# One core, a long convolution beside a token-mixing MLP: order of the sine table, taps in one evacuation, inverse table after the last gelu, even products in place

## The chip, the cores and the metric

The kernel runs on one core of a Trainium2 chip. The metric is the device time of one execution in microseconds (us), lower is better. Engines are named as in the profile: PE (matrix multiply), PEld (its weight loads), DVE (vector), ACT (activation), POOL (GpSimd), SP (the queue that issues most transfers).

## What is computed

Sequence length S = 2048, width D = 640, F = 1536, bf16 inputs. Path A is an H3-like layer: a short causal convolution of k (4 taps per channel), times v, then a long convolution over the sequence with one filter per channel (written with FFTs), plus a skip term, times q. Path B is a layer norm of x = q over D, a two-layer MLP over the sequence axis with a tanh-gelu, and a transpose back. A gate per token, g = sigmoid(sum(x * gate_w)), blends them.

```python
k_shift = sum over t of k_pad[:, t:t + S, :] * shift_k[:, ks - 1 - t]
kv = k_shift * v
y  = irfft(rfft(kv padded to 2S) * rfft(ssm_k padded to 2S))[:S] + kv * ssm_D
a  = q * y
u  = gelu(einsum("bsd,sf->bdf", layernorm(x), w1) + b1)
b  = (einsum("bdf,fs->bds", u, w2) + b2) transposed
out = g * a + (1 - g) * b
```

## The kernel before

**Long convolution.** It is done with real trigonometric tables and matrix products. The sequence is split in two halves h and, inside each, in four residues p. The table FTB (slices p = 0 to 3, 128x1024 each) holds sines and cosines. The arguments are made by integer arithmetic on DVE into `pint` (L791 to L796: a product, an add of 1024, an AND with 4095, for each p in the order 0, 2, 1, 3) and go through `Sin` on ACT (L797). `pint` lies on the memory of ring[1]; the k tiles `kn` and `kp` use the same bytes later.

**Filter.** `transp(h, db)` (L826) turns the filter block by block on PE against an identity; ACT evacuates each block into `wT` (L837). The skip term ssm_D is folded in by one row product per block (Drow). Then `fwd` (L839) multiplies `wT` by the table for each p, and ACT evacuates into C[0] (h = 0) and C[1] (h = 1). `mixing` (L869) combines the four residues on DVE.

**Short convolution.** The taps are laid out by a DVE copy "taps" (L789) from the small load `rows`, transposed by four tiny PE products (L808 to L810), and copied into `cw` by four ACT instructions, one per group of 32 partitions (L812). POOL multiplies `cw` with a mask `m32` into the shift table KF (L944, four instructions). k is turned by transposing DMAs into KT, and `kv` (L971) multiplies KT by KF on PE; the result times v is the signal.

**Signal.** `fwd_even` (L853) transforms the signal's residues p = 0 and 2: eight PE products, each evacuated by ACT ("Ae", L861) into a temporary buffer Th, from which three DVE instructions (L865 to L867) make all slots of the target for p = 0 and 2. `fwd` does p = 1 and 3. The signal's first half goes to C[2] with C[1] as the temporary (L999), the second to C[3] with C[2] (L1006). C[1] holds the filter's second half until its mixing is done.

**MLP.** Layer-norm statistics on DVE, their power step on POOL (L904 to L908), the normalisation on DVE (L913). m1 products (L1025 on) accumulate over the sequence for 12 column tiles ft; ACT applies the gelu into GT (L1039). m2 products (L1065 on) are evacuated by ACT into O1 (L1084).

**Inverse.** The inverse table is made from FTB: four transposing DMAs into GTB (L1060), then four ACT copies in place over FTB (L1061, "gil"). Spectral products run on DVE (`cross`, `product`), then `invmix`, and `inverse` (L1171) on PE, whose evacuation and the blend with O1 end the kernel.

**What sets the order.** Nothing is ordered by hand. Every instruction is added to `_Sched` (L324) with an engine, an estimated duration and a priority (its index in program order unless `prio` is given; lower goes first). `run` (L384) simulates the engines with these estimates and takes, on each free engine, the ready instruction with the lowest priority number. `emit` then issues in that order, and each engine runs its own list strictly in order. A dependency is found from overlapping memory regions; `after` lets an operation be taken only once another has started in the simulation. An evacuation's dependencies are handed to the first PE product of its group (L370 to L376). PSUM is cut into four slots of two banks; MLP groups may hold two of them, convolution groups three. SP, ACT ("QA") and POOL issue transfers; most on SP are chained in program order.

```python
            if e in ("SP", "QA") or op.lat < 0:
                issue = 1.2 if e == "POOL" else 0.1
                s = max(t + issue, dma_free)
                dma_free = s + op.dur
                op.end = dma_free + 2.0 + (6.0 if e == "POOL" else 0.0)
```

Of the kernel before, what the change touches and what calls it, by code (L numbers as in the profile page):

```python
# [323 lines left out]
class _Sched:  # L324
# [59 lines left out]
    def run(self):  # L384
# [12 lines left out]
        pend = {e: [] for e in engs}  # L397
        free = {e: 0.0 for e in engs}
        port = {"DVE": 0.0, "POOL": 0.0}
# [111 lines left out]
def _build(nc, A_q, A_k, A_v, A_shift_k, A_ssm_k, A_ssm_D, B_x, B_w1, B_b1, B_w2, B_b2, gate_w, out):  # L511
# [10 lines left out]
    with ExitStack() as es:  # L522
# [13 lines left out]
        def alloc(name, shape, dtype, at=None):  # L536
            size = mybir.dt.size(dtype)
            for s_ in shape[1:]:
                size *= s_
            if at is None:  # L540
                off = cur[0]
                cur[0] = (off + size + 63) // 64 * 64
            else:
                off = at
            assert off % 4 == 0 and off + size <= top, f"SBUF overflow {name}: {off}+{size} > {top}"
            h = nc.alloc_sbuf_tensor_at(name, list(shape), dtype, offset=off)
            T.reg_sbuf(h, off)
            return h
# [46 lines left out]
        ksh = [alloc(f"ksh{i}", [128, 4, D], BF16, at=base_of(GT) + 5120 * (1 + i)) for i in range(2)]  # L595
        rows = alloc("rows", [20, 4, 512], BF16, at=base_of(GT))
        kn = [alloc(f"kn{i}", [128, 4, D], BF16, at=base_of(ring[1]) + 5120 * i) for i in range(2)]
# [21 lines left out]

        def tt(eng, o, a, b, op, mode=2, prio=None):  # L620
            n = n_of(o)
            d = dve_dur(n, mode) if eng == "DVE" else n / 600.0 + 0.17
            o_ = SC.add(eng, d, lambda s: T.op(eng, lambda e: e.tensor_tensor(o, a, b, op), [a, b], [o]),  # L623
                        [a, b], [o], prio=prio, name="tt")
            o_.lock = True
            return o_
# [138 lines left out]
        small(Drow[:, :], dr(A_ssm_D, 0, [[0, 1], [1, D]]), 1280, "QA")  # L765
        small(rows[0:20, 0, 0:128], dr(A_shift_k, 0, [[128, 20], [1, 128]]), 5120, "QA")
        small(rows[0:4, 1, :], dr(B_b2, 0, [[512, 4], [1, 512]]), 4096, "QA")
        small(rows[0:12, 2, 0:128], dr(B_b1, 0, [[128, 12], [1, 128]]), 3072, "QA")
        for a, b in SSM0:
            ssm_load(0, a, b)  # L770
        for hk in range(4):
            x_load(hk)
        for a, b in SSM1:
            ssm_load(1, a, b)
# [11 lines left out]
        ts("DVE", ident[:, :], dif[:, :], 0.0, None, ALU.is_equal)  # L786
        memset("POOL", cw[:, :, :], 0.0)
        ro, ri = rows[0:20, 3, :].rearrange("g (j q c) -> g j q c", j=4, q=4), V(rows, 0, [[1, 4], [0, 4], [4, 32]], pn=20)
        SC.add("DVE", 0.6, lambda s: T.op("DVE", lambda e: e.tensor_copy(ro, ri), [ri], [ro]), [ri], [ro], prio=0, name="taps")  # L789
        PORD = (0, 2, 1, 3)  # L790
        for p in PORD:  # L791
            pv = pint[:, p, :, 1, :]
            tt("DVE", pv, V(acol, p, [[4, 2], [0, 256]]), V(brow, 0, [[0, 2], [1, 256]]), ALU.mult, mode=1)
            ts("DVE", pint[:, p, :, 0, :], pv, 1024.0, None, ALU.add, mode=2)
            pa = pint[:, p, :, :, :].rearrange("q a b c -> q (a b c)")
            ts("DVE", pa, pa, 4095, None, ALU.bitwise_and, mode=2)  # L796
            act(FTB[:, p, :, :, :, :].rearrange("q a b c d -> q (a b c d)"), pa, ACT.Sin, bias=cst[:, 0:1],  # L797
                scale=-(2.0 * math.pi / 4096.0) * (1.0 - 1e-6), name="sin")
# [8 lines left out]
        items = []  # L807
        for j in range(4):  # L808
            items.append(((lambda s, j=j: s[:, 512 + 20 * j:512 + 20 * j + 20]), rows[0:20, 3, 128 * j:128 * j + 128], ident[0:20, 0:20], True, True))
        mms(vt, items, prio=0, name="cst")  # L810
        for q in range(4):
            act(V(cw, q, [[7, NG], [1, 4]], p0=32 * q, pn=32), (lambda s, q=q: s[32 * q:32 * q + 32, 512:592].rearrange("p (j g) -> p g j", j=4)), ACT.Copy, vt=vt, prio=0, name="cw")  # L812
        b2f = V(cc, 0, [[1, 4], [4, 4]])
        ts("DVE", dif2[:, :], dif2[:, :], 31, None, ALU.bitwise_and, mode=2)
        ts("DVE", m32[:, :], dif2[:, :], 0.0, None, ALU.is_equal, mode=2)

# [9 lines left out]
        def transp(h, db):  # L826
            vt = _VT("cv")
            items = []
            for kt in range(2):
                for p in range(4):  # L830
                    o = (lambda s, j=4 * kt + p: s[:, 128 * j:128 * j + 128])
                    dfold = h == 0 and kt == 0 and p == 0
                    if dfold:
                        items.append((o, ident[0:1, :], Drow[0:1, 128 * db:128 * db + 128], True, False))
                    items.append((o, V(ssm, db * S + 1024 * h + 4 * kt + p, [[8, 128]]), ident[:, :], not dfold, True))
            mms(vt, items, name="wtr")
            act(V(wT, 2 * h * SL + 128 * db, [[SL, 2], [D, 4], [1, 128]]), (lambda s: s[:, :].rearrange("q (a b c) -> q a b c", a=2, b=4)), ACT.Copy, vt=vt, name="wT")  # L837

# [13 lines left out]

        def fwd_even(src, h, dst, Th, Ts):  # L853
            pos = {(0, 0, 0): 0, (0, 0, 1): 1, (0, 1, 0): 2, (0, 1, 1): 3, (2, 0, 1): 4, (2, 1, 0): 5, (2, 1, 1): 6, (2, 0, 0): 7}
            for p in (0, 2):
                for kt in range(2):
                    for c in range(2):
                        vt = _VT("cv")
                        items = [(chk(ci), FTB[:, p, kt, c, 0, :], src(kt, p, ci), True, True) for ci in range(2)]
                        mms(vt, items, name="A")  # L860
                        act(V(Th, Ts * SL + D * pos[(p, kt, c)], [[320, 2], [1, 320]]), two, ACT.Copy, vt=vt, name="Ae")  # L861

            def t4(o, n, dims):
                return V(Th, Ts * SL + D * o, dims + [[1, n]])
            tt_("DVE", V(dst, 0, [[2 * D, 2], [1, D]]), t4(0, 2 * D, []), t4(2, 2 * D, []), ALU.add)  # L865
            tt_("DVE", V(dst, 2 * SL + 2 * D, [[-2 * D, 2], [1, D]]), t4(4, 2 * D, []), t4(6, 2 * D, []), ALU.add)
            tt_("DVE", V(dst, D, [[2 * SL, 2], [2 * D, 2], [1, D]]), t4(0, D, [[4 * D, 2], [D, 2]]), t4(2, D, [[4 * D, 2], [D, 2]]), ALU.subtract)  # L867

# [24 lines left out]
        def ln_tile(hk, p):  # L893
            t = 4 * hk + p
            xs = X[:, hk, p, :]
            ops = []
            for ci in range(2):
                o, i = stats[:, t, 6 * ci:6 * ci + 6], xs[:, 320 * ci:320 * ci + 320]
                ops.append(SC.add("DVE", 0.38, (lambda o, i: lambda s: T.op("DVE", lambda e: e.bn_stats(o, i), [i], [o]))(o, i), [i], [o]))  # L899
            o, i = mv[:, t, :], stats[:, t, :]  # L900
            ops.append(SC.add("DVE", 0.12, (lambda o, i: lambda s: T.op("DVE", lambda e: e.bn_aggr(o, i), [i], [o]))(o, i), [i], [o]))
            return ops
# [14 lines left out]
        LNA = 8  # L917
        lnlast = []
        KFP = (0, 5, 10, 15)
        srcW = lambda h: (lambda kt, p, ci: wT[:, 2 * h + kt, p, 320 * ci:320 * ci + 320])  # L920
        for h in range(2):
            for db in range(ND):
                transp(h, db)
            if h == 0:
                consts()
            for p in PORD:
                fwd(srcW(h), h, p, C[h], p, 1.0 / 1024.0, "W", (lambda c, k2: False) if h == 0 else (lambda c, k2: c == 1))
            if h == 0:
# [14 lines left out]
                for g0 in KFP:  # L943
                    tt("POOL", KF[:, g0:g0 + 20 // len(KFP), :, :], V(cw, 7 * g0, [[7, 20 // len(KFP)], [1, 7], [0, 32]]), V(m32, 0, [[0, 20 // len(KFP)], [0, 7], [1, 32]]), ALU.mult)  # L944
                for hk in range(2):
# [52 lines left out]
        srcA = lambda kt, p, ci: vkv0[:, kt, p, 320 * ci:320 * ci + 320]  # L998
        fwd_even(srcA, 0, C[2], C[1], 0)  # L999
        for p in (1, 3):  # L1000
# [4 lines left out]
        srcB = lambda kt, p, ci: kv1[:, kt, p, 320 * ci:320 * ci + 320]  # L1005
        fwd_even(srcB, 1, C[3], C[2], 0)  # L1006
        for p in (1, 3):
# [51 lines left out]
        for p in range(4):  # L1059
            dma(GTB[:, p, :, :, :, :].rearrange("q a b c d -> q (a b c) d"), FTB[:, p, :, :, :, :].rearrange("q a b c d -> q (a b c) d"), 128 * 2048, rate=200.0, transpose=True, prio=10 ** 5)  # L1060
            act(V(FTB, 1024 * p, [[1, 2], [256, 4], [2, 128]]), V(GTB, 1024 * p, [[512, 2], [128, 4], [1, 128]]), ACT.Copy, prio=10 ** 5, name="gil")  # L1061

# [196 lines left out]
```

## Time and profile before

| | us |
|---|---|
| median of 5 runs | 189.63 |
| lowest to highest | 189.56 to 190.79 |
| the profiled execution | 189.56 |
| its span in the profile | 187.0 |
| busy PE / DVE / ACT / POOL | 173.0 / 168.8 / 119.2 / 37.0 |

The profile shows one execution. Its page gives busy time by engine and the span in 40 slices of 4.7 us, where a digit is the busy share in tenths. A row of a timeline is: start, duration, engine, line, operation, result <- operands, shapes, count, and in brackets the idle time of that engine just before with what ended it. All PE products stand at L293, all ACT functions at L667, DVE's two-operand arithmetic at L623: these are helpers, so rows are told apart by tile names, in which buffer numbers are left out (C is any of C[0] to C[3]). An ACT row at L667 without tiles is a table load.

In order of time: the first filter block is on PE at 3.50, the first forward product at 15.98, the first gelu at 39.14, the first short-convolution product at 47.7, the signal's transforms at 57.2 to 95.8, the last gelu at 114.57, m2 from 114.4, the first inverse product at 156.75, and the last DVE instruction at 184.30. SP issues the k loads at 12.24, and the ring loads behind them at 13.87.

### The profile page before, as it was taken

Reading aid. Unit: us, or ns where it says so; the run is one execution under the profiler, and the core shown is the slowest. Engines: PE = TensorE matmul, PEld = TensorE weight load, DVE = VectorE, ACT = ScalarE, POOL = GpSimd, SP = SyncE. Lnnn points to the kernel's source line nnn. Section 1 sums busy time; section 2 is a strip of 40 time slices with the busy share of each in tenths; the row PEclk is TensorE's granted clock in tenths of the full one; section 3 lists DMA queues with packets and bytes.
Section 4 is the critical chain, followed back from the end, with each engine's and each line's share of the span. In section 5 each row is a group of like instructions: output and inputs, shape, how many; then the busy total and the mean of one; then the engine's idle time right before and its main releaser. Section 6 shows DMA issues by size and latency. Waiting matters only on the chain.

```text
span 187.0 us, 3316 instructions
## 1 busy us (share of the span) xinstructions
PE 173.0 (93%) x1374; PEld 129.3 (69%) x1374; DVE 168.8 (90%) x199; ACT 119.2 (64%) x180; POOL 37.0 (20%) x41
## 2 busy tenths in 40 slices
PE   3746999989999999999979999999999999999994
PEld 2523667757877876767747777888888887778672
DVE  7999795999599954999999999999999999969974
ACT  2996989599978999999797111221313134563760
POOL 2089304000001540000011530200204031252000
PEclk9999999999999999999999999999999999999999
DMA  5999999999991999990799699956958999999463
GB/s 164 399 413 367 390 227 230 359 404 211 190 350 52 214 204 241 237 178 6 143 236 255 108 193 158 342 108 200 314 106 249 297 204 227 273 200 229 139 212 138
DMA packets 38206, 42.85 MB, mean 229 GB/s; under 512 B 15787, under 2 KB 31280, under 8 KB 38192
## 3 DMA queue, kind: packets, MB, share of 16 engines
q1 hardware_dynamic: 33200, 32.15, 57.5%
q0 software_dynamic: 4928, 10.49, 31.6%
q8 instruction: 10, 0.16, 0.3%
q14 instruction: 4, 0.03, 0.0%
q10 hardware_dynamic: 64, 0.01, 0.0%
HBM read 25.87 MB, written 2.62 MB: 152 GB/s over the span
## 4 chain that ended last, share of the span: by engine, by line
PE 81%; ACT 15%; DMA 1%; issue 1%; DVE 0%
PE pp L293 81%; ACT C L667 4%; ACT wT L667 4%; ACT FTB L667 3%; ACT ksh L667 2%; DMA ssm<-in_A_ssm_k_dram 1%; ACT L667 1%; ACT GT L667 1%; ACT cw L667 0%; DVE O L679 0%; ACT gth L667 0%
## 5 line engine op out<-in xcount | busy, mean ns | idle before, releaser
L623 DVE TENSOR_TENSOR C<-C 128x2560 bf16<-128x2560 bf16 (+2 forms) x34 | 52.2, 1564 | 6.1 <-ACT C L667 6.1
L293 PE MATMUL pp<-X,ring 128*128 128x320 bf16 x384 | 55.4, 299 | 1.5 <-ACT GT L667 1.2
L293 PE MATMUL pp<-GT,W 128*128 128x320 bf16 x384 | 52.8, 299 | 0.0
L293 PEld LDWEIGHTS pp<-GT,W 128*128 128x128 bf16 x384 | 43.4, 114 | 8.8 <-ACT cgb L667 0.2
L293 PEld LDWEIGHTS pp<-X,ring 128*128 128x128 bf16 x384 | 37.2, 98 | 16.5 <-issue 1.9
L667 ACT ACTIVATE C<-pp 128x640 bf16<-128x640 f32 x64 | 40.2, 720 | 5.6 <-PE pp L293 5.6
L667 ACT ACTIVATE O<-pp,c,omg 128x640 bf16<-128x640 f32 x15 | 13.3, 886 | 34.7 <-PE pp L293 34.7
L293 PE MATMUL pp<-wT,FTB 128*128 128x320 bf16 x128 | 20.6, 315 | 2.2 <-ACT wT L667 1.4
L262 POOL DMA_DIRECT2D C<-C x8 | 9.9, 1359 | 46.6 <-DVE C L623 46.4
L293 PEld LDWEIGHTS pp<-wT,FTB 128*128 128x128 bf16 x128 | 12.2, 102 | 9.4 <-ACT wT L667 1.5
L667 ACT ACTIVATE GT<-pp,cc 128x640 bf16<-128x640 f32 x12 | 9.5, 791 | 13.0 <-PE pp L293 12.9
L262 POOL DMA_DIRECT2D C<-q_hi x6 | 5.9, 984 | 54.5 <-DVE C L623 27.6
L667 ACT ACTIVATE cgb<-pp,gg 128x640 bf16<-128x640 f32 x16 | 12.7, 794 | 5.7 <-PE pp L293 5.7
L623 DVE TENSOR_TENSOR tm<-C,C 128x2560 bf16<-128x2560 bf16 (+1 forms) x7 | 14.4, 2056 | 0.0
L899 DVE BATCH_NORM_STATS2 stats<-X 128x6 f32<-128x320 bf16 x32 | 13.4, 461 | 0.4 <-DMA X<-in_A_q_dram 0.4
L293 PE MATMUL pp<-C,FTB 128*128 128x320 bf16 x96 | 13.7, 299 | 0.0
L623 DVE TENSOR_TENSOR C<-tm 128x2560 bf16<-128x2560 bf16 (+1 forms) x10 | 12.0, 1218 | 0.0
L293 PEld LDWEIGHTS pp<-C,FTB 128*128 128x128 bf16 x96 | 8.9, 98 | 4.2 <-ACT O L667 0.4
L667 ACT ACTIVATE gq<-gq 128x640 bf16<-128x640 bf16 x16 | 11.8, 748 | 0.0
L623 DVE TENSOR_TENSOR SS<-C 128x2560 bf16<-128x2560 bf16 x8 | 11.7, 1489 | 0.1
L293 PE MATMUL pp<-ident,ssm 128*128 128x128 bf16 x80 | 8.4, 270 | 3.3 <-DMA ssm<-in_A_ssm_k_dram 2.2
L667 ACT ACTIVATE wT<-pp 128x1024 bf16<-128x1024 f32 x10 | 9.7, 1029 | 1.0 <-PE pp L293 1.0
(69 smaller groups left out, 183.7 us busy)
## 6 DMA issues: line engine op xcount, KB each, us to landing
ring<-in_B_w_dram SPq DMA_DIRECT2D x12, 512.0 KB, 11.9
W<-in_B_w_dram SPq DMA_DIRECT2D x8, 768.0 KB, 7.2
C<-C POOLq DMA_DIRECT2D x8, 640.0 KB, 10.1
X<-in_A_q_dram SPq DMA_DIRECT2D x4, 640.0 KB, 8.1
kn<-in_A_k_dram SPq DMA_DIRECT2D x4, 640.0 KB, 9.5
out_dram<-O SPq DMA_DIRECT2D x7, 320.0 KB, 2.8
ssm<-in_A_ssm_k_dram SPq DMA_DIRECT2D x3, 512.0 KB, 5.6
vkv<-in_A_v_dram SPq DMA_DIRECT2D x2, 640.0 KB, 5.0
```

Source lines behind the costliest of these rows:

```text
L262: ins = engobj.dma_start(out_ap, in_ap, accum_op=ALU.add, max_dma_last_dim=2560)
L293: ins = self.nc.tensor.matmul(ps_ap, lhsT=lhsT, rhs=rhs, start=start, stop=stop, skip_group_check=True)
L623: o_ = SC.add(eng, d, lambda s: T.op(eng, lambda e: e.tensor_tensor(o, a, b, op), [a, b], [o]), [a, b], [o], prio=prio, name="tt")
L667: return T.op("ACT", lambda e: e.activation(o, src, func, **kw), rr + [src], ww)
L899: ops.append(SC.add("DVE", 0.38, (lambda o, i: lambda s: T.op("DVE", lambda e: e.bn_stats(o, i), [i], [o]))(o, i), [i], [o]))
```

## The change

1. The planner lets ACT start at 2.0 us instead of 0. The filter evacuation of block 0 comes after the start of sine 0, and those of the other blocks of h = 0 after the start of sine 2. Sines 1 and 3 get priorities among the evacuations of the first forward transform.
2. The argument arithmetic goes slice by slice: a slice's product is taken only after the AND of the slice before has started. The first layer-norm statistic comes after the last AND has started.
3. The tap copy writes a sparse layout (`rows` gets a fifth row, cleared by POOL instead of `cw`), seven PE products transpose it, and one ACT instruction of 128x140 fills all of `cw`. The mask's two small DVE steps get priority 0.
4. The tap load moves from ACT's queue to SP's, between the second and third filter load; the two bias loads move to SP's behind the x loads.
5. The first KF product on POOL also names the last slice of `pint` as read, so it comes behind the arithmetic; the other three come after its start.
6. `fwd_even` evacuates into slots 1 and 3 of its own target instead of Th, and the three DVE instructions read them there.
7. The four inverse-table copies come after the last gelu has started.

```diff
-        free = {e: 0.0 for e in engs}
+        free = {e: 2.0 if e == "ACT" else 0.0 for e in engs}
...
-        rows = alloc("rows", [20, 4, 512], BF16, at=base_of(GT))
+        rows = alloc("rows", [20, 5, 512], BF16, at=base_of(GT))
...
-        small(rows[0:20, 0, 0:128], dr(A_shift_k, 0, [[128, 20], [1, 128]]), 5120, "QA")
-        small(rows[0:4, 1, :], dr(B_b2, 0, [[512, 4], [1, 512]]), 4096, "QA")
-        small(rows[0:12, 2, 0:128], dr(B_b1, 0, [[128, 12], [1, 128]]), 3072, "QA")
-        for a, b in SSM0:
+        for a, b in SSM0[:2]:
+            ssm_load(0, a, b)
+        small(rows[0:20, 0, 0:128], dr(A_shift_k, 0, [[128, 20], [1, 128]]), 5120, "SP", chain=True)
+        for a, b in SSM0[2:]:
             ssm_load(0, a, b)
         for hk in range(4):
             x_load(hk)
+        small(rows[0:4, 1, :], dr(B_b2, 0, [[512, 4], [1, 512]]), 4096, "SP", chain=True)
+        small(rows[0:12, 2, 0:128], dr(B_b1, 0, [[128, 12], [1, 128]]), 3072, "SP", chain=True)
...
-        memset("POOL", cw[:, :, :], 0.0)
-        ro, ri = rows[0:20, 3, :].rearrange("g (j q c) -> g j q c", j=4, q=4), V(rows, 0, [[1, 4], [0, 4], [4, 32]], pn=20)
+        memset("POOL", rows[0:20, 3:5, :].rearrange("g a b -> g (a b)")[:, 0:896], 0.0)
+        ro, ri = V(rows, 1536, [[128, 4], [160, 4], [1, 32]], pn=20), V(rows, 0, [[1, 4], [0, 4], [4, 32]], pn=20)
...
-            tt("DVE", pv, V(acol, p, [[4, 2], [0, 256]]), V(brow, 0, [[0, 2], [1, 256]]), ALU.mult, mode=1)
+            t_ = tt("DVE", pv, V(acol, p, [[4, 2], [0, 256]]), V(brow, 0, [[0, 2], [1, 256]]), ALU.mult, mode=1)
...
-            ts("DVE", pa, pa, 4095, None, ALU.bitwise_and, mode=2)
-            act(FTB[:, p, :, :, :, :].rearrange("q a b c d -> q (a b c d)"), pa, ACT.Sin, bias=cst[:, 0:1],
+            if p != 0:
+                t_.after.add(pprev)
+            pprev = ts("DVE", pa, pa, 4095, None, ALU.bitwise_and, mode=2)
+            pv3 = pa
+            sins[p] = act(FTB[:, p, :, :, :, :].rearrange("q a b c d -> q (a b c d)"), pa, ACT.Sin, bias=cst[:, 0:1],
...
-        for j in range(4):
-            items.append(((lambda s, j=j: s[:, 512 + 20 * j:512 + 20 * j + 20]), rows[0:20, 3, 128 * j:128 * j + 128], ident[0:20, 0:20], True, True))
+        for j in range(7):
+            items.append(((lambda s, j=j: s[:, 512 + 20 * j:512 + 20 * j + 20]), V(rows, 1536 + 128 * j, [[1, 128]], pn=20), ident[0:20, 0:20], True, True))
         mms(vt, items, prio=0, name="cst")
-        for q in range(4):
-            act(V(cw, q, [[7, NG], [1, 4]], p0=32 * q, pn=32), (lambda s, q=q: s[32 * q:32 * q + 32, 512:592].rearrange("p (j g) -> p g j", j=4)), ACT.Copy, vt=vt, prio=0, name="cw")
+        act(cw[:, :, :], (lambda s: s[:, 512:652].rearrange("p (j g) -> p g j", j=7)), ACT.Copy, vt=vt, prio=0, name="cw")
...
+            if h == 0:
+                o_.after.add(sins[0 if db == 0 else 2])
...
-                        act(V(Th, Ts * SL + D * pos[(p, kt, c)], [[320, 2], [1, 320]]), two, ACT.Copy, vt=vt, name="Ae")
...
+                        act(V(dst, SL * (1 + p) + D * (pos[(p, kt, c)] % 4), [[320, 2], [1, 320]]), two, ACT.Copy, vt=vt, name="Ae")
+
+            tt_("DVE", V(dst, 0, [[2 * D, 2], [1, D]]), V(dst, SL, [[D, 2], [1, D]]), V(dst, SL + 2 * D, [[D, 2], [1, D]]), ALU.add)
+            tt_("DVE", V(dst, 2 * SL + 2 * D, [[-2 * D, 2], [1, D]]), V(dst, 3 * SL, [[D, 2], [1, D]]), V(dst, 3 * SL + 2 * D, [[D, 2], [1, D]]), ALU.add)
+            tt_("DVE", V(dst, D, [[2 * SL, 2], [2 * D, 2], [1, D]]), V(dst, SL, [[2 * SL, 2], [D, 2], [1, D]]), V(dst, SL + 2 * D, [[2 * SL, 2], [D, 2], [1, D]]), ALU.subtract)
...
+                if h == 0 and p in (1, 3):
+                    sins[p].prio = SC.ops[-1].idx - (16.5 if p == 1 else 8.5)
...
-                    tt("POOL", KF[:, g0:g0 + 20 // len(KFP), :, :], V(cw, 7 * g0, [[7, 20 // len(KFP)], [1, 7], [0, 32]]), V(m32, 0, [[0, 20 // len(KFP)], [0, 7], [1, 32]]), ALU.mult)
+                    tt("POOL", KF[:, g0:g0 + 20 // len(KFP), :, :], V(cw, 7 * g0, [[7, 20 // len(KFP)], [1, 7], [0, 32]]), V(m32, 0, [[0, 20 // len(KFP)], [0, 7], [1, 32]]), ALU.mult, xr=[pv3] if g0 == 0 else []).after.update(kfirst[:1])
+                    kfirst.append(SC.ops[-1])
...
-            act(V(FTB, 1024 * p, [[1, 2], [256, 4], [2, 128]]), V(GTB, 1024 * p, [[512, 2], [128, 4], [1, 128]]), ACT.Copy, prio=10 ** 5, name="gil")
+            act(V(FTB, 1024 * p, [[1, 2], [256, 4], [2, 128]]), V(GTB, 1024 * p, [[512, 2], [128, 4], [1, 128]]), ACT.Copy, prio=10 ** 5, name="gil").after.add(g_)
```

## The prediction, made before the result was known

> **What bounds the kernel now.** I read the page's busy lines, then the chain that ended last, then the timeline of each engine where the chain leaves PE. The page first.
>
> ```profile
> span 187.0 us, 3316 instructions
> ...
> PE 173.0 (93%) x1374; PEld 129.3 (69%) x1374; DVE 168.8 (90%) x199; ACT 119.2 (64%) x180; POOL 37.0 (20%) x41
> ...
> PE   3746999989999999999979999999999999999994
> ...
> ACT  2996989599978999999797111221313134563760
> ...
> PE 81%; ACT 15%; DMA 1%; issue 1%; DVE 0%
> ```
>
> PE is nearly full from slice 5 on. The stretches view gives it 6.98 us of work in the first 15.98, 15.31 of the next 15.45, and 59.71 of 59.71 from 96.99 to 156.70. So the time is PE's fixed work plus its holes. The holes are 9.0 us before 15.98, 0.8 near 39, 1.2 near 96 and the tail. The chain, in order of time, says who makes the first one:
>
> ```profile
> 4.74 0.91 issue
> 5.65 1.28 ACT L667
> 6.93 0.01 issue
> 6.94 2.20 ACT FTB L667 x2
> ...
> 10.09 1.02 ACT wT L667
> 11.11 2.08 ACT FTB L667 x2
> 13.19 2.75 ACT wT L667 x3
> 15.94 0.05 issue
> 15.98 10.66 PE pp L293 x64
> ```
>
> From 4.61 to 15.98 ACT never rests: a table load, four sines, four tap copies, and five evacuations of the transposed filter (wT), all of which the first forward transform needs. PE's own timeline shows the other side:
>
> ```profile
> 5.82 1.07 PE L293 MATMUL pp<-ident,ssm 128*128 128x128 bf16 x8 [1.03 <-DMA ssm<-in_A_ssm_k_dram]
> ...
> 10.12 0.65 PE L293 MATMUL pp<-ident,ssm 128*128 128x128 bf16 x4 [1.10 <-ACT cw L667]
> ...
> 15.98 4.28 PE L293 MATMUL pp<-wT,FTB 128*128 128x320 bf16 x19 [1.44 <-ACT wT L667]
> ```
>
> PE stands still for ACT between 8.3 and 15.98 in four pieces (1.10, 0.40, 1.79, 1.44 us). The second hole, from the timeline of 60 to 105 us:
>
> ```profile
> 94.86 1.35 ACT L667 ACTIVATE FTB<-GTB 128x1024 bf16<-128x1024 bf16 x1
> ...
> 96.07 0.77 ACT L667 ACTIVATE GT<-pp,cc 128x640 bf16<-128x640 f32 x1
> ...
> 96.99 8.31 PE L293 MATMUL pp<-X,ring 128*128 128x320 bf16 x60 [1.18 <-ACT GT L667]
> ```
>
> A reorder of the inverse table stands ahead of a gelu whose two PSUM banks PE needs.
>
> **The sines and the table load.** Before, ACT loads a table for the first wT copy (2.31) and a second one for the sines at 5.65. No later copy needs a load until the gelu at 37.85, so copies run under the sine table. With a sine first, one load of 1.28 us is left. The row stands against the Trainium skill, ScalarE: Activation LUTs, What ACT_TABLE_LOAD costs, which puts a switch at about 2.66 us, because a drain of about 1.38 follows the load. Here the load ends at 6.93 and the sine starts at 6.94: no drain. By the rule this part is worth 2.66, by the row 1.28; I take the row. The load can begin at about 1.25, since only Drow's issue (0.73 + 0.52) stays on ACT's queue.
>
> The first sine then waits for its table argument. DVE did slices 0 and 2 interleaved from 1.51 to 4.68, 3.17 us, so one slice costs 1.6. Slice after slice, the first is ready at 3.1, and the sine (1.14) runs to about 4.3, inside ACT's present wait of 1.02 before the first wT at 4.61. The second is ready at 4.7 and its sine runs at 5.6 to 6.7, after that wT. PE's transposes of the next block end at 6.9 as before, so neither sine is on the path. Without that cover a sine costs its 1.1.
>
> **The taps.** Four copies of 32x80 (1.01 us) become one of 128x140. Rows near it are 128x28 at 0.213 and 128x512 at 0.608, hence about 0.30: 0.7 off ACT, and PE's 1.10 wait for cw shrinks. PE transposes seven tap pieces instead of four (0.28 us): about 0.2 more. The clearing memset on 20 partitions instead of 128x140 (0.21) is hidden on an idle POOL.
>
> The tap load leaves ACT's queue and goes on SP's between the second and third filter load. Here a rule speaks against the change. The Trainium skill, DMA: Bandwidth & Descriptors, Queues, rings and completion order, says that SP and ACT each own a row of rings, served in turn, and that one row is consumed in order. On its own row the load had landed before the DVE copy at 5.20, which shows no wait. On SP's it lies behind 768 KB, which landed at about 5.8 (the release of 5.82 above). DVE reaches the copy after two slices and one product, at about 5.4 to 6.0. So by the row of before its cost is 0, by the rule up to 0.6 us of DVE in a fixed order, with the last two slices behind it. These feed sines needed only at 12 us, and cw at about 8.7. I take 0 on the path. On SP's queue the small issue (0.31) puts off the third filter load and everything behind it by as much, and the two bias loads (0.66) put off the second half of the filter and the w1 loads by about 1 us together. The queue is backlogged (409 GB/s from 5 to 10 us, 399 from 10 to 16) and these are used after 24 us: 0.
>
> **When the first transform starts.** With these off ACT, PE paces the transposes: one block of eight plus its Drow product starts every 1.22 us (5.82, 7.04). Four blocks from 5.82 plus 0.45 for the taps end at 11.15; the last wT copy (1.02) ends at 12.2. That is 3.8 before 15.98.
>
> **The sines that moved back.** Sines 1 and 3 (1.14 each) now stand among the sixteen evacuations of that transform. The first falls into the 1.25 us in which ACT waited at 17.27 for the first sums: nothing. The other goes into a run that ACT bounds (eleven evacuations in 6.67 us): +1.1, less up to 0.67, the two waits of 0.36 and 0.31 that it may fill. Behind sine 1 on SP's queue stand the k loads (their buffers overlay slices 0 to 2), two w1 loads and the gate weights. They were issued at 12.24 when that sine ended, and it now ends at about 13.2: up to 1 us later, used at 22 us and later, 0. ACT's last evacuation and the five wT copies of the second half end at 33.20 now, and 2.7 to 3.3 earlier then. I take **3.0**. PE has fed itself from 31.43 on, so its full stretch starts 3.0 earlier.
>
> **Shift table behind the arithmetic.** The four POOL products (KF, 2.06 each) now wait for the last slice, ready at about 8.5. They wait for cw anyway (10.20 before, about 9.4 then). The variance step queued behind them on POOL moves from 18.31 to about 17.6, and the normalised X 0.7 earlier. PE asks for X's second half at 34.70, which becomes 31.7; it is ready at 31.97 less 0.7. That just fits, and I count 0. It is worth 0.7 at most; if it fails, rival 1.
>
> **The inverse table behind the last gelu.** Four copies of 1.37 leave 87 to 101 us and run after 115, where ACT waits 2.37 us before each output evacuation (887 ns per 3.26). Two fit before the first such wait ends, none is needed before the inverse at 156.6, and their transposes are not moved. In the new place: 0, at worst 0.6 if all four stand in one row ahead of an evacuation whose banks PE needs. In the old place the hole of 1.18 goes. Between 0 and 1.2 I take **1.0**, since the next evacuation can be late too.
>
> **Even products in place.** The even products are evacuated into the odd slots of their own target instead of another buffer. Counts and sizes stay. A wait goes and a wait comes:
>
> ```profile
> 71.23 0.82 DVE L623 TENSOR_TENSOR C<-C 128x1280 bf16<-128x1280 bf16 x1 [2.57 <-ACT C L667]
> ...
> 73.64 2.23 DVE L623 TENSOR_TENSOR C<-C 128x1280 bf16<-128x1280 bf16 x2 [1.58 <-ACT C L667]
> ...
> 77.19 2.82 DVE L623 TENSOR_TENSOR C<-C 128x5120 bf16<-128x5120 bf16 x1
> ```
>
> The even products no longer wait for C1, whose mixing ends at 64.8. The odd ones wait until three DVE combinations (0.82, 0.82, 1.49 us) have read the odd slots. They are queued on DVE behind C1's mixing; PE's cover meanwhile is the m1 products. DVE's 4.15 us of waits above may fall to 0; the 77.19 step may also slip. PE is full there, so on the path I take 0. Bounds: 0.5 gained to 1.5 lost, the latter in rival 3.
>
> **Sum.** The profiled execution took 189.56: its span of 187.0 and 2.56 around it; the median of the runs is 189.63, so no correction. 189.56 - 3.0 - 1.0 = **185.6**. DVE's chain can give way to PE: at the end PE has 24 m2 products (3.45 us, from 180.81) behind the last inverse, and DVE's start at 48.79 (a wait of 1.93 for the second half's evacuations) moves up by some 2.6.
>
> **Rivals.** 1: the gain of the head stops at another supply. The normalised X moves only 0.7 (POOL's power step of 1.68 stands behind KF), so PE waits where X or w1 comes in: 189.56 - 0.7 - 1.0 = **187.9**. For: DVE waits 2.12 for rstd at 30.50. Against: PE's request is matched to within a microsecond.
> 2: it doesn't do what it says. The sine isn't first, or a load still stands before the copies: 1.28 of the 3.0 comes back and the second hole moves to another gelu: 189.56 - 1.7 = **187.8**. Against: no load stands before the copy at 9.05.
> 3, slower: the in-place wait. If the combinations get behind the v products and C1's mixing, the sixteen evacuations of the A transform end late, and DVE's mixing of C2, now at 77.19, with them. From there DVE is full to 156.36. PE covers 3.45 less about 1.1 for the last evacuation; so from a start later than 79.5 the end slips one for one. Combinations at 70 and eight odd evacuations at half of ACT's share (1.3 each) give 80.5 to 81, **190.8**. For: ACT is full at 60 to 90 us (30.0 of 30). Against: the even evacuations move up by as much as the odd ones move back.
>
> **Chances.** The sum 0.66 (its own range 184.0 to 187.2: head 2.0 to 4.0 with PE's slow early pace ending sooner or later, reorder 0 to 1.2, in place 0.5 to -0.4), rival 1 0.09, rival 2 0.06, rival 3 0.14, and 0.05 for small holes that eat all of it. About 0.5% (0.95 us) is what a measurement here can tell from no change. Faster 0.80, same 0.06, slower 0.14. The range 183.7 to 189.2 takes in the two weak gains and leaves out rival 3.
>
> **What would show it.** Two table loads instead of three; the first forward transform at about 12.2 instead of 15.98; the second half's last wT copy ending near 30.2; one cw copy of about 0.30; no hole near 96 with the four reorders after the last gelu; C2's mixing before 79.5. Wrong if PE shows a new hole between 25 and 40, or DVE a start of C2's mixing behind 80.

## The result, and the profile after

| | before | after |
|---|---|---|
| median, us | 189.65 (80 runs) | 188.58 (43 runs) |
| ratio, 95% interval | 1 | 0.9929 (0.9914 to 0.9943) |
| profiled execution, us | 189.56 | 187.95 |
| its span, us | 187.0 | 185.8 |

The change makes the kernel about 1.35 us faster (0.0071 of 189.65). The ratios, here and below, leave out executions that fell into a slower state, which the medians include, so the quotient of the medians is not the ratio. The forecast was 185.6: the direction was right, and the gain is a third of the 4.0 us that were forecast. The helpers of the kernel after stand one line further on (L668 for L667, L624 for L623, L680 for L679).

A trace is one execution, and PE's pace in the first forward transform is not the same in all. The run of 23 products that stands at 12.21 below took 5.23 us in the kernel after and from 4.45 to 5.97 us in the eight traces that have the new head. So a start in one trace less the same start in another is good to about 1 us up to there; lengths within one trace are better.

The page of the kernel after, first its busy lines and then the chain that ended last:

```profile
span 185.8 us, 3318 instructions
...
PE 174.4 (94%) x1377; PEld 129.1 (70%) x1377; DVE 169.3 (91%) x199; ACT 117.8 (63%) x176; POOL 38.0 (20%) x41
...
PE 44%; DVE 26%; ACT 14%; DMA 10%; issue 4%; POOL 0%; SPq 0%; DVEq 0%
```

The last line is the news. Before, PE carried 81% of the chain and DVE 0%; now PE has 44%, DVE 26% and transfers 10%. Something other than PE sets the end. The busy lines could not have told it: they hardly moved.

**The head.** ACT's timeline of the kernel after:

```profile
1.27 1.28 ACT L668 ACT_TABLE_LOAD   x1 [1.27 <-PEq L1256]
3.44 1.15 ACT L668 ACTIVATE FTB<-pint,cst 128x1024 bf16<-128x1024 int32 x1 [0.89 <-DVE pint L638]
...
8.20 0.29 ACT L668 ACTIVATE cw<-pp 128x140 bf16<-128x140 f32 x1 [1.48 <-PE pp L293]
...
26.10 4.69 ACT L668 ACTIVATE wT<-pp 128x1024 bf16<-128x1024 f32 x5 [0.59 <-PE pp L293]
```

One table load at 1.27, the first sine before the first wT copy, one tap copy of 0.29: as forecast. The second half's wT copies end at 26.10 + 4.69 = 30.79 (33.20 before). PE's timeline of the kernel after, from the first forward product to the short convolution:

```profile
11.29 0.45 PE L293 MATMUL pp<-wT,FTB 128*128 128x320 bf16 x1 [0.39 <-ACT wT L668]
12.21 5.23 PE L293 MATMUL pp<-wT,FTB 128*128 128x320 bf16 x23 [0.47 <-ACT wT L668]
...
20.20 4.28 PE L293 MATMUL pp<-wT,FTB 128*128 128x320 bf16 x28 [0.65 <-ACT C L668]
...
32.70 1.31 PE L293 MATMUL pp<-wT,FTB 128*128 128x320 bf16 x8 [0.25 <-ACT C L668]
34.21 0.72 PE L293 MATMUL pp<-wT,FTB 128*128 128x320 bf16 x4 [0.20 <-ACT C L668]
...
45.07 1.10 PE L293 MATMUL pp<-KF,KT 128*128 128x128 bf16 x19
```

One product is at 11.29; the run starts at 12.21 (forecast 12.2), 3.77 earlier than before. At 20.20 PE waits for an evacuation behind sine 3: the lead shrinks to 2.4 at the last wT copy. From 31.19 twenty filter products stand in a row, and PE waits for ACT's evacuations twice. Before, 64 filter products and 32 X products lay between 33.62 and 47.71; now 64 and only 24 lie between 31.19 and 45.07. The short convolution starts 2.64 earlier, but eight X products (1.09 us by the row of 8 every 1.09) are still to be done: a net lead of 1.55. Over all traces the short convolution starts between 43.84 and 46.39 with the new head (eight, median 45.47) and between 47.66 and 48.95 with the old (seven, median 47.98). That is 2.51 apart, or 1.4 net.

**The middle.** The hole near 96 is gone. From 45.07 to 111.34 the stretches view has PE busy for 66.27 of 66.27; before, 65.33 of the 66.66 from 47.71 to 114.37. m2 starts at 111.34, 3.03 earlier than before.

**The end.** Only 1.15 of the 3.03 is left at the last instruction (184.30 before, 183.15 after). DVE's timeline of the kernel after:

```profile
162.88 1.49 DVE L624 TENSOR_TENSOR SS<-C 128x2560 bf16<-128x2560 bf16 x1 [2.41 <-DMA C<-C]
...
183.15 0.55 DVE L680 SCALAR_TENSOR_TENSOR O<-pp,omg,cgb 128x320 bf16<-128x320 f32 x1 [1.06 <-PE pp L293]
```

PE's timeline of the kernel after:

```profile
168.79 4.54 PE L293 MATMUL pp<-C,FTB 128*128 128x320 bf16 x32 [1.45 <-DVE C L624]
...
177.52 5.60 PE L293 MATMUL pp<-GT,W 128*128 128x320 bf16 x40
```

The chain of waits, just before that:

```profile
147.81 0.73 POOL C L262
148.54 14.25 DMA C<-C
...
162.88 1.49 DVE SS L624
```

DVE's mixing of the last half needs the second of two transfers that add one SBUF region into another (C<-C, 640 KB, issued by POOL). It takes 14.25 us and lands at 162.79. DVE waits 2.41, PE 1.45 for DVE, with 40 m2 products still queued behind the inverse. Before, the same mixing waited for no transfer. DVE's timeline of the kernel before:

```profile
165.45 0.82 DVE L623 TENSOR_TENSOR q_hi<-cgb,q_hi 128x1280 bf16<-128x1280 bf16 x1 [1.92 <-ACT cgb L667]
166.25 1.50 DVE L623 TENSOR_TENSOR SS<-C 128x2560 bf16<-128x2560 bf16 x1
```

### The profile page after: what moved, and what is told of

It reads as the page before. It is cut to its first block, busy times and chain, and to the rows that moved or that the text cites. A ratio compares the mean times of both kernels' runs of the same rounds, so it can differ in the third digit from the quotient of the medians.

```text
span 185.8 us, 3318 instructions
## 1 busy us (share of the span) xinstructions
PE 174.4 (94%) x1377; PEld 129.1 (70%) x1377; DVE 169.3 (91%) x199; ACT 117.8 (63%) x176; POOL 38.0 (20%) x41
## 4 chain that ended last, share of the span: by engine, by line
PE 44%; DVE 26%; ACT 14%; DMA 10%; issue 4%; POOL 0%; SPq 0%; DVEq 0%
PE pp L293 44%; DVE C L624 15%; DMA C<-C 8%; DVE tm L624 8%; ACT C L668 5%; ACT gq L668 5%; DVE q_hi L624 3%; DMA ssm<-in_A_ssm_k_dram 2%; ACT wT L668 2%; ACT GT L668 1%; DVE SS L624 1%; ACT L668 1%; ACT FTB L668 1%; POOL C L262 0%; DVE O L680 0%
## 5 line engine op out<-in xcount | busy, mean ns | idle before, releaser
L624 DVE TENSOR_TENSOR C<-C 128x2560 bf16<-128x2560 bf16 (+2 forms) x34 | 51.7, 1565 | 0.1
L668 ACT ACTIVATE C<-pp 128x640 bf16<-128x640 f32 x64 | 40.6, 718 | 6.3 <-PE pp L293 6.3
L668 ACT ACTIVATE O<-pp,c,omg 128x640 bf16<-128x640 f32 x15 | 13.2, 883 | 29.1 <-PE pp L293 29.0
L293 PE MATMUL pp<-wT,FTB 128*128 128x320 bf16 x128 | 21.8, 321 | 2.8 <-ACT C L668 1.1
L668 ACT ACTIVATE GT<-pp,cc 128x640 bf16<-128x640 f32 x12 | 9.6, 800 | 14.2 <-PE pp L293 14.2
L668 ACT ACTIVATE cgb<-pp,gg 128x640 bf16<-128x640 f32 x16 | 12.7, 794 | 8.6 <-PE pp L293 5.6
L624 DVE TENSOR_TENSOR tm<-C,C 128x2560 bf16<-128x2560 bf16 (+1 forms) x7 | 14.3, 2058 | 0.0
L624 DVE TENSOR_TENSOR SS<-C 128x2560 bf16<-128x2560 bf16 x8 | 11.7, 1489 | 2.6 <-DMA C<-C 2.6
L624 DVE TENSOR_TENSOR C<-tm 128x2560 bf16<-128x2560 bf16 (+1 forms) x10 | 12.0, 1220 | 0.1
L668 ACT ACTIVATE gq<-gq 128x640 bf16<-128x640 bf16 x16 | 11.7, 742 | 0.0
L624 POOL TENSOR_TENSOR KF<-cw,m 128x1120 bf16<-128x1120 bf16 x4 | 8.1, 2060 | 9.4 <-ACT wT L668 9.4
```

Of the source, the lines that this page charges most:

```text
L293: ins = self.nc.tensor.matmul(ps_ap, lhsT=lhsT, rhs=rhs, start=start, stop=stop, skip_group_check=True)
L668: return T.op("ACT", lambda e: e.activation(o, src, func, **kw), rr + [src], ww)
```

## The experiments

The question is where 4.0 became 1.35. The expectations name theories by letters and say beside each what it predicts. In short, A puts the loss into the head (X comes late, the tap load on SP's queue delays DVE), C puts it at the end (the accumulating transfer, slowed by the loads of q beside it, takes back what was gained); the rivals are stated where they stand. Every ratio is against the kernel before on the same chip.

| run | what it is | us | ratio (95% interval) |
|---|---|---|---|
| head_only | before + parts 1 to 5 | 188.75 | 0.9953 (0.9915 to 0.9990) |
| gil_only | before + part 7 | 189.18 | 0.9976 (0.9939 to 1.0012) |
| inplace_only | before + part 6 | 203.41 | 1.0685 (1.0633 to 1.0737) |
| before_nohead | before + parts 6, 7 | 194.82 | 1.0239 (1.0188 to 1.0290) |
| after_noinplace | parts 1 to 5, 7 | 189.36 | 1.0000 (0.9974 to 1.0026) |
| after_nogil | parts 1 to 6 | 190.38 | 1.0049 (1.0017 to 1.0081) |
| tap_act | after, tap load on ACT's queue | 189.46 | 0.9971 (0.9930 to 1.0013) |
| ln_behind | after, all statistics behind the last AND | 197.91 | 1.0390 (1.0336 to 1.0444) |
| qlo_late | after, later loads of q's second half | 186.79 | 0.9863 (0.9821 to 0.9905) |
| before_qlo | before, the same | 189.45 | 0.9989 (0.9961 to 1.0018) |
| nohead_qlo | parts 6, 7, the same | 193.17 | 1.0208 (1.0150 to 1.0266) |
| gate_early | nohead_qlo, gate products first | 188.22 | 0.9924 (0.9894 to 0.9954) |
| qlo_gate | qlo_late, gate products first | 186.24 | 0.9830 (0.9798 to 0.9863) |

**One part alone.** The edits are those of the diff above, cut to the parts named.

head_only: 

> The kernel before with parts 1 to 5 of the change alone (sines, taps, small loads, shift table), neither the in-place products nor the moved inverse table. Theory A, the head's gain stops at the normalised X: the first forward product is at 12.2 us as in the whole change, X comes about 2 us later than before, the first gelu stays at 39.2 (39.0 to 39.6), and the gain is 1.0 to 2.0 us: 187.6 to 188.6. Rival B, the head keeps its 3.0 us and the other two parts lose it: first gelu at 36 to 37.5, 186.6.

gil_only: 

> The kernel before with the inverse table's four copies behind the last gelu, alone. Theory A: the hole of 1.18 us on PE near 96 goes and nothing takes its place: 188.5. Rival B: PE runs ahead of DVE by as much, and a hole of about the same size comes at the last inverse products: 189.5.

inplace_only: 

> The kernel before with the even products in place, alone. Theory A: C2's mixing starts 3 to 6 us earlier on DVE (71 to 74 instead of 77.2), PE is full there anyway, so the time is 189.2 to 189.8, and the only gain possible is the hole at 96 that may move. Rival B: the in-place wait costs PE or ACT time: a new hole of PE between 50 and 75, 190.3 or more.

head_only is 0.5% faster, less than either theory said. Its short convolution is at 43.84, 3.87 before that of the kernel before, with the same eight X products short: 2.78 net in this trace, against 1.55 in the kernel after. PE's pace makes part of the difference (4.45 us for the 23 products, 5.23 there). Its first gelu is at 37.97, between the two forecasts. The hole near 96 stays (1.19), a new PE hole of 1.55 comes at 68.63, and one of 0.98 at 171.50.

gil_only is not told from no change, and neither theory describes it. PE's timeline of gil_only, two rows, then the end of DVE's:

```profile
96.71 17.55 PE L293 MATMUL pp<-X,ring 128*128 128x320 bf16 x128 [0.16 <-ACT GT L667]
...
182.11 1.79 PE L293 MATMUL pp<-GT,W 128*128 128x320 bf16 x12
```

```profile
184.82 1.01 DVE L679 SCALAR_TENSOR_TENSOR O<-pp,omg,cgb 128x320 bf16<-128x320 f32 x2
```

The hole near 96 shrinks to 0.16, and from the short convolution to m2's start it takes 65.63 us instead of 66.66. The end takes this back. The planner leaves 12 m2 products behind the last inverse instead of 24, so PE is done at 183.90 and DVE only at 185.83. From m2's start to the end of DVE's last instruction it is 71.74 us, before 70.48.

inplace_only is 6.9% slower, which neither theory said; why, is taken up below.

**The tap load.**

```diff
+        small(rows[0:20, 0, 0:128], dr(A_shift_k, 0, [[128, 20], [1, 128]]), 5120, "QA")
         for a, b in SSM0[:2]:
             ssm_load(0, a, b)
-        small(rows[0:20, 0, 0:128], dr(A_shift_k, 0, [[128, 20], [1, 128]]), 5120, "SP", chain=True)
```

> The whole change, with the tap load alone put back on ACT's queue. Theory A, the small load between the filter loads is what makes X late: DVE's first statistic starts at 8.7 to 9.2 instead of 10.27, X is normalised from 31 instead of 32.5, the first gelu is at 38.2 or earlier, and the time falls by 0.5 to 1.2 against the whole change (187.4 to 188.0). Rival B: X's landing is what the memory gives in a run and does not follow the tap load: first statistic at 10 again, time as the whole change (188.4).

Its median is above that of the kernel after, not below: the move to SP's queue isn't the loss. Its first statistic is at 9.44; with the load on SP's queue it is at 10.27 (after), 9.88 (head_only) and 9.35 (qlo_late), so X's landing doesn't follow the tap load. Its first gelu is at 39.91, not earlier. DVE's wait for the taps is 0.33 in the kernel after, 0.54 in qlo_late, 1.11 in ln_behind.

**Late X.**

```diff
-            if t == 0:
-                ops[0].after.add(pprev)
+            for o_ in ops:
+                o_.after.add(pprev)
```

> The whole change; every layer-norm statistic, not the first alone, is put behind the start of the last table AND. Theory A2, X is late because DVE's last table arithmetic (1.1 us) and with it KF stand behind a statistic that waits for X: the last AND ends by 9.5 instead of 12.1, KF starts by 9.7 instead of 12.24, X's second half is normalised from 31.0 to 31.8 instead of 32.53, and PE gains 0.3 to 1.0 before 45 us; the end may take it back (ratio 0.987 to 0.993). Rival: X follows its landing alone, normalised at 32.2 or later although KF is early; ratio 0.993.

X is ready earlier, as planned: its second half is normalised at 30.77 (32.53 after). The first gelu (39.29, after 39.20) and the short convolution (45.16, after 45.07) don't move; from the row of filter products at 31.28 (31.19 after) to the short convolution it is 13.88 us in both. So late X doesn't set the head's lead, and A falls. What remains is the order that the planner wrote (twenty filter products in a row) and ACT's pace there; this is read from the trace and wasn't tried by itself. The time missed both forecasts. The 3.9% loss has another place: PE waits 8.49 us behind an output evacuation, which stands behind a table copy that waits for a transpose (below).

**The loads of q's second half.** In program order they stand ahead of the inverse and were issued at 150.08 us, 2 us behind the accumulating transfers. Here they also name a product of q's first half as read, and so come behind it. No engine's order changes: the two traces have the same sequence on every engine and queue.

```diff
-        for kt in range(2):
-            dma(q_lo[:, kt, :, :], ..., 128 * 5120).after.add(w2last)
         Z0 = invmix(A0[0], A0[1], C3a, None, None)
         inverse(0, Z0)
+        for kt in range(2):
+            dma(q_lo[:, kt, :, :], ..., 128 * 5120, xr=[q_hi[:, :, 2, :]]).after.add(w2last)
```

> The whole change; the two loads of q's second half, issued at 150 us while the last two accumulating transfers run, are made to wait for a q product of the first inverse (they read as a dependency what it writes), so they start near 158. The order of every engine is that of the whole change. Theory C, the end is lost in the accumulating transfer, which shares the transfer engines: it lands 3 us or more sooner than the 14.25 us of the whole change, DVE's wait of 2.41 before the last mixing goes, PE's hole of 1.45 at 168.8 goes, and the time falls by 1.0 to 1.5 against the whole change (ratio to before 0.985 to 0.988). Rival D, the accumulate is slow by itself (12 us or more without q's loads beside it): DVE's wait and the hole stay, ratio 0.993; if q's loads then come too late, DVE waits at 172.9 for them instead.

186.79 us, faster than both kernels. DVE's timeline of qlo_late shows the mixing that had waited:

```profile
161.11 1.49 DVE L624 TENSOR_TENSOR SS<-C 128x2560 bf16<-128x2560 bf16 x1
```

It has no wait, and PE has no hole from m2's start to its last product. The view of the tile C, for POOL's instructions from 146 to 160 us, gives the times of its two transfers from issue to landing, first in the kernel after, then in qlo_late:

```profile
DMA to landing us min/median/max: 10.6/12.4/14.2
```

```profile
DMA to landing us min/median/max: 8.6/9.8/11.0
```

The slower of the two lands in 11.0 us instead of 14.2 when 1.28 MB of loads are no longer under way beside it. From m2's start to the last instruction it is 182.32 - 112.05 = 70.27 us here, 183.15 - 111.34 = 71.81 in the kernel after, 184.30 - 114.37 = 69.93 before. C holds.

Are these loads just badly placed in any kernel? 

> The kernel before with one edit: the loads of q's second half issue only behind the spectral products of q's first half, as in the run that moved them in the kernel after. Every engine keeps its order. Theory C (the wait of DVE's last mixing for an accumulating transfer took the gain at the end, and the kernel before has no such wait because PE is the late one there): no change, ratio 0.997 to 1.002. Rival D (these loads cost time by themselves, whatever the kernel): about 1.5 us faster, ratio about 0.992.

0.9989: no change, as C said. In the kernel before the second transfer was issued at 153.2 and took 13.0 us by the same view, so it landed at 166.2, just as DVE came to the mixing (166.25). In the kernel after it is issued 4.6 us earlier, but DVE is ready for the mixing 5.8 us earlier, at 160.47, and takes longer to get it. That is how the transfer became a bound.

**One part taken out.**

after_noinplace: 

> The whole change without the in-place even products (parts 1 to 5 and the moved inverse table). Theory C: DVE's work from 80 us on is as in the kernel before, the last mixing is bound by the accumulate, and the end is within 0.8 us of the whole change: ratio 0.990 to 0.997. Rival: the in-place products cost as much as they give, then this is faster than the whole change by 0.8 or more: ratio below 0.989.

after_nogil: 

> The whole change with the inverse table's copies left at their old priority, ahead of the last gelus. In-place alone lost 13 us because the table's transposes on SP's queue waited for ACT's sums and stood ahead of the second layer's weights, while a table copy on ACT waited for a transpose ahead of a gelu. Theory: the same cycle comes here, 10 to 15 us slower than before (ratio 1.05 to 1.08), so the moved table is what makes the in-place products usable. Rival: with the new head the order falls out differently and the loss is below 3 us.

Without the in-place products nothing is left of the gain (1.0000); both theories missed. PE's timeline of after_noinplace:

```profile
69.74 1.25 PE L293 MATMUL pp<-X,ring 128*128 128x320 bf16 x8 [1.54 <-ACT GT L668]
```

It is the hole of head_only again: four gate sums stand ahead of that gelu on ACT from 65.88 on. The kernel after, where the planner puts these sums later, has none there. The end costs too, as in gil_only: 12 m2 products are left behind the last inverse, and from m2's start to the end of DVE's last instruction it is 71.74. In this change the in-place products are worth more than the 0 forecast. Without part 7 the change is 0.5% slower than before: far from the 10 to 15 us of the theory, and within the rival's loss of less than 3. ACT's timeline of after_nogil, then PE's:

```profile
109.09 1.35 ACT L668 ACTIVATE FTB<-GTB 128x1024 bf16<-128x1024 bf16 x1 [8.32 <-DMA GTB<-FTB]
```

```profile
111.13 4.52 PE L293 MATMUL pp<-X,ring 128*128 128x320 bf16 x32 [3.17 <-ACT GT L668]
```

A table copy stands ahead of a gelu and waits for a transposing transfer; PE waits for the gelu.

**The old head with the in-place products.**

before_nohead: 

> The kernel before with parts 6 and 7 only (even products in place, inverse table behind the last gelu); the head is the old one. Theory C: the end hangs on DVE's chain and on the accumulating transfers, and much of the head's gain is lost there, so leaving the head out costs less than the head's 1.6 us of earlier short convolution: ratio 0.990 to 0.998, a wait of DVE for the transfer at the end that is shorter than the 2.41 us of the kernel after. If the head's gain reaches the end whole: 1.6 us slower than the kernel after, ratio about 1.001.

nohead_qlo: 

> Parts 6 and 7 with the old head, and the later loads of q's second half. Theory C: with the transfer out of the way the end follows PE again, so the head's gain shows whole between this kernel and the one with all seven parts and the later loads (186.8 us): this one takes about 188.3, ratio about 0.994, without a wait of DVE for an accumulating transfer. If the head's gain is lost elsewhere too: within 0.5 us of 186.8, ratio about 0.987.

Both missed. On the old head parts 6 and 7 cost 2.4%, not a fraction of a per cent gained, and the later loads don't mend it. SP's timeline of nohead_qlo, and PE's:

```profile
95.46 3.41 SPq L260 DMA_TRANSPOSE GTB<-FTB  x1
98.91 1.40 SPq L267 DMA_DIRECT2D W<-in_B_w_dram  x1
100.36 19.06 SPq L260 DMA_TRANSPOSE GTB<-FTB  x3
119.52 12.71 SPq L267 DMA_DIRECT2D W<-in_B_w_dram  x4
```

```profile
118.79 42.38 PE L293 MATMUL pp<-GT,W 128*128 128x320 bf16 x300 [2.65 <-DMA W<-in_B_w_dram]
```

Before, the four transposes went out from 79.10 to 92.71, ahead of all W2 loads, and landed in a median of 3.2 us. They write memory that the gate buffers `gq` also use, so they wait for the gate sums. ACT's last gate sum ended at 90.07 before and at 88.92 in after_noinplace, but at 98.97 here and at 98.68 in the kernel after: with part 6 the planner puts the gate products later on DVE. The transposes then go out among W2 loads and accumulating transfers, land late (median 10.7 us, at most 19.3), and the W2 loads behind them on SP's queue wait too. inplace_only shows the same at 100.45 us (20.57 us for three; this execution took 206.47), with PE holes of 1.72 and 8.41 behind table copies and one of 3.75 for a W2 load. To take this cause away, the gate products go first on DVE:

```diff
-                    tt("DVE", gb[:, :, :], X[:, hk, 2 * a:2 * a + 2, :], V(gwb, 0, [[0, 2], [1, D]]), ALU.mult)
+                    tt("DVE", gb[:, :, :], X[:, hk, 2 * a:2 * a + 2, :], V(gwb, 0, [[0, 2], [1, D]]), ALU.mult, prio=1)
```

gate_early: 

> Parts 6 and 7 on the old head with the later loads of q's second half (193.2 us in the run before), and the eight gate products first on DVE. If late gate sums are what holds up the table's transposes and, behind them on SP's queue, the second filter loads of the MLP: the transposes land before 100 us, all W2 loads issue early enough, the 2.65 us wait of PE for a W2 load goes, and the time falls to 188 to 189.5 us. If the loss lies in the in-place products themselves (their waits on the old head): it stays at 192 to 194 us.

qlo_gate: 

> All seven parts, the later loads of q's second half (186.8 us), and the eight gate products first on DVE, so that the transposes stand ahead of the first W2 loads on SP's queue. With the new head no engine waited for these transposes, so by the same theory: no gain, 186.3 to 187.3 us. If transposes among the accumulating transfers still cost something in the kernel after: up to 1 us faster, 185.8.

SP's timeline of gate_early:

```profile
84.88 5.51 SPq L260 DMA_TRANSPOSE GTB<-FTB  x4
90.43 36.78 SPq L267 DMA_DIRECT2D W<-in_B_w_dram  x6
```

The transposes take 5.51 us, the W2 loads follow from 90.43, PE has no hole there, and 193.17 becomes 188.22. From m2's start to the end of DVE's last instruction 74.68 us become 70.59, which is most of it. So the loss was not in the in-place products' own waits. (The edit also moves other DVE steps; the transposes are what the waits name.) On the new head the same edit gives 186.24. Its interval overlaps that of qlo_late: no gain that can be told. The two runs of this pair shared the chip, and differ by the head alone: 188.22 against 186.24. With the end cleared, the head is worth 2.0 us, and parts 6 and 7 with the two repairs 1.4.

## Why the prediction was right or wrong

- **Head: mechanism right, size too large (3.0 forecast, 1.55 net at the short convolution, 1.4 by the medians of all traces).** The start at 12.2, the one table load and the one tap copy came out as worked out. Two terms were mis-sized. Sine 3 was put at 1.1 less waits that it might fill, so that 3.8 would become 3.0; the lead went from 3.77 to 2.4 over its stretch, with a PE hole of 0.65 behind it. And "PE has fed itself from 31.43 on, so its full stretch starts 3.0 earlier" took PE's stretch as fixed: moved earlier, it met ACT's pace and put eight X products (1.09 us) off. That ACT's pace and the planner's row of filter products do this is read from the trace and not shown by a run. With the end cleared, the head measured 2.0 us.
- **"The normalised X 0.7 earlier": wrong sign.** The first half's POOL chain starts at 20.35 instead of 18.31, 2 us later. The wait was overlooked: statistics for which X wasn't there yet (landed at 10.27) stand ahead of the last AND on DVE (part 2 holds back only the first of them), and KF waits for that AND and then starts at 12.24 instead of the 9.4 forecast. It cost nothing, as ln_behind shows; rival 1 named this supply and is refuted as the bound.
- **Tap load, 0: right,** as far as tap_act can tell. DVE does wait for the taps (0.33 to 1.11 us in the traces), but not on the path.
- **Inverse table, 1.0: right as to the hole, not as time.** The hole is gone, and no output evacuation is late. Alone it gains nothing that can be told: PE's 1.03 us are lost at the end, where 12 m2 products are left instead of the 24 that the forecast counted on. And the forecast's "their transposes are not moved" was wrong: with part 6 they went from 79.10 to 95.15. In the whole change part 7 is needed for that: without it the change is slower.
- **In place, 0 on the path: wrong in both directions.** Rival 3's price was a late mixing of C2; it ran at 70.6, 6.6 earlier than before. The in-place products remove a hole of 1.54 which the head opens, and they bring DVE's chain forward (the next to last mixing at 153.30; 155.44 in after_noinplace, 156.36 before). In a different order (inplace_only, before_nohead) they cost 2 to 7% by a way that no case named: gate sums, transposes, W2 loads.
- **The step that failed: "DVE's chain can give way to PE".** It was argued from what DVE computes and when it starts, and from the 24 m2 products left at the end. The start at 48.79 did not move up by 2.6; the planner put it behind two v products, at 52.25. And what DVE waits for was not asked: the accumulating transfer. Of 3.03 us at m2's start 1.88 went between there and the end. With the loads beside it moved, the loss is 0.34 (70.27 against 69.93), and the time 186.8.
- **What each is worth.** Of the 4.0 us forecast 1.35 came. The later loads bring about 1.25 more (ratio 0.9863 against 0.9929), which is shown. The other 1.4 is about what the head falls short by (1.55 for 3.0), which is read from the traces.

## What to carry to other kernels

A lead gained early must be followed through every wait down to the end; a transfer that lands just in time before a change is the next bound after it, and what shares the transfer engines with it can be moved. Where a planner writes the order, an edit that costs nothing by itself can shift the release of shared memory (here gate sums) and so reorder a queue somewhere else; compare each queue's order before and after, not only the instructions edited. And when parts are tried alone, their gains don't add up: here one of them costs 6.9% alone and is needed in the whole, and another closes a hole of PE and gives the gain back at the end.

## What the runs showed of the hardware that was not expected

A hole of PE can cost more than itself. Stretches view of ln_behind, whose PE stood still from about 118 to 126.48:

```profile
core 0: us, PE busy (x) PEld busy (x) DVE busy (x) ACT busy (x) POOL busy (x), PEclk, DMA share, GB/s
...
126.50:131.00 4.50, 4.50 (x18) 2.54 (x18) 4.40 (x4) 1.91 (x2) 1.20 (x1) 0.50 1.07 261
...
140.00:150.00 10.00, 10.00 (x76) 8.34 (x75) 10.00 (x7) 2.65 (x3) 2.76 (x3) 1.00 1.07 257
```

After the hole the granted clock is 0.50 for 4.5 us: 18 products where 34 would fit at the later rate of 76 in 10 us, some 2.1 us lost on top of the hole's 8.49. inplace_only shows the same after its hole of 8.41 (0.66, 27 products in 5.4 us), and nohead_qlo even after one of 2.65 (0.54, 13 products in 3.2 us). But after_nogil has a hole of 3.17 and a clock of 1.00 behind it, so these runs give no length from which on it happens. The kernel after, whose largest hole behind the head is 1.45, has a granted clock of 1.00 there. The Trainium skill (TensorE: Matmul & The Clock Gate, Part 1: The HAM clock gate) puts the idle clock at half and has it return after some 4 us of work; the trace of ln_behind agrees (0.50, for 4.5 us).
